# A linear-attention block with a gated FFN on one core: another search for the order of the instructions, and the last sum in two halves of columns

## The chip, the cores and the metric

The kernel runs on one core of a Trainium2 chip. The time is the device time of one execution in microseconds (us); the median of three runs before the change is 631.77 us (631.66 to 632.82). The core has a matrix engine (TensorE, in rows PE, its weight loads PEld), VectorE (DVE), ScalarE (ACT), GpSimd (POOL), and SyncE (SP), whose queue issues all DMA transfers. Every engine works off its own instructions in a fixed order, and waits at the first one whose inputs aren't ready.

## The reference

With x of 2048 tokens by 512, xn = layernorm(x), 32 heads of 16, F = 1792, all float32:

```
q, k, v = split(xn @ wqkv);  phi(t) = where(t > 0, t + 1, exp(t)) + 1e-6
kv = phi(k)^T v per head;  z = sum of phi(k) over the tokens
s = (phi(q) kv / (phi(q) z + 1e-6)) @ wo
g = silu((gelu(xn @ w_gate) * (xn @ w_up)) @ w_down)
out = x + s * g
```

## The kernel before, in words

**Products.** Each float32 product is computed as three matmuls on operands split into a rounded high part and a low part (hi·hi, hi·lo, lo·hi: `mm3`, L362 to L366). The high part is a cast on ScalarE (L350), the low part a subtraction, mostly on VectorE (L356). Block products are done in a seven-product form with fewer products and more sums; the sums of x blocks (`forms`, tiles T0 to T7) and of weight blocks (`prep_w`, tiles tmp) are GpSimd additions of 128x256, those of outputs (c, u, e) VectorE additions.

**Stages.** Tokens come in 16 tiles of 128 rows, taken in pairs (0 with 4, 1 with 5, and so on). From 0 to about 100 us: load x and wqkv, layernorm (`ln`, L496: statistics st, mv and ve on VectorE, rstd on GpSimd, xn on VectorE), transposition on TensorE (pt, L522), high and low parts of x (Xh, Xl) and of weights (kq, a21, b12), then k and q. phi of k (kp) and of q (qp) is made from two ScalarE steps and a VectorE step (L591); q goes to DRAM (q_d), and xn^T phi(k) is summed up in four PSUM banks (gps). The first raw FFN weights (raw0, raw1) and the spills of Xh and Xl to DRAM (xh_d, xl_d) go over the same SP queue from about 40 us on. Then the FFN runs for the second half of the tokens (FX, FY, FZ; fu, h, hh, hl; the down sums d into acc), the attention of all tiles follows at 356 to 410 us (u = phi(q)·z on GpSimd, den and its reciprocal rr and pn on VectorE, ptq by transposition, pqTh on ScalarE, pqTl on VectorE, sps = 12 products a tile), then the FFN of the first half. Its last down sums (`down`, L868) end the kernel: per j of 8, 12 products into one PSUM bank of 128x512, an addition to acc (L885), silu (L895), a multiplication with s (L1069), an addition of x, and a transfer out (`finish0`, L1060). Already before, j=7 did the steps behind the products in two halves of 256 columns; the sums of x for j < 6 were GpSimd's.

**What sets the order.** The program states the operations once. Its class `Plan` gives each a cost, finds what it depends on (tiles, PSUM banks, buffer places), and lists them: `forward` (L205) walks in time and takes on each engine the ready operation with the smallest due time `late`; TensorE's operations are bound to a stated order within 6 us. Due times come from eight passes back from the end (`latest`, L178). After that 400 rounds (`ROUNDS`, L19 and L134) each draw a wait of TensorE, shift the due times of operations around it at random, list again, and keep what ends sooner by the planner's own account. That account holds one port that GpSimd operations and VectorE operations without PSUM operands take in turns, and one DMA line at 260 KB/us with 1.5 us on top. The order so found is what each engine gets.

Of the kernel before, what the change touches and what calls it, by code (L numbers as in the profile page):

```python
# [18 lines left out]
ROUNDS = 400  # L19
# [50 lines left out]
class Op:  # L70
    __slots__ = ("eng", "cost", "lat", "fn", "pre", "suc", "key", "late", "end", "left", "ready", "name", "turn", "port", "kb", "lat0")


class Plan:

    AHEAD = 6.0
    RATE = 260.0
# [5 lines left out]
    def do(self, eng, cost, fn, out, *ins, more=(), lat=0.0, key=None, name="", kb=0):  # L83

        op = Op()
        op.eng, op.cost, op.lat, op.key, op.name = eng, cost, lat + self.HOP[eng], key, name
# [24 lines left out]
        for p in op.pre:  # L111
            p.suc.append(op)
        self.ops.append(op)
        return op

    def order(self, pe_keys):
        rank = {k: i for i, k in enumerate(pe_keys)}
        pe = sorted((o for o in self.ops if o.eng == "PE"), key=lambda o: rank[o.key])
        now = 0.0
        for o in pe:  # L120
            o.turn = now
            now += o.cost
# [10 lines left out]
        draw = random.Random(1)  # L133
        for n in range(ROUNDS):  # L134
            end, done, late = best
            for o in self.ops:
                o.late = late[o]
            waits = self.waits(done)
            at = draw.choices([w[0] for w in waits], [w[1] for w in waits])[0]
            back, share, far = draw.uniform(1.0, 12.0), draw.choice((0.05, 0.2, 0.5)), draw.uniform(0.2, 4.0)  # L140
# [3 lines left out]
            done = self.forward(pe)  # L144
            end = max(t for t, _ in done)
            if end <= best[0]:
                best = end, done, {o: o.late for o in self.ops}
        return [o for _, o in best[1]]

    @staticmethod  # L150
    def waits(done):

        out, last = [], 0.0
        for t, o in done:
            if o.eng == "PE":
                if t - o.cost - last > 0.02:
                    out.append((o.late, t - o.cost - last))
                last = t
        out.append((last, max(t for t, _ in done) - last - 4.0))
        return out  # L160
# [44 lines left out]
    def forward(self, pe):  # L205
# [8 lines left out]
        done, first = [], 0  # L214
        while any(cands.values()):
# [3 lines left out]
            for e, c in cands.items():  # L219
# [46 lines left out]
def kernel(  # L266
# [52 lines left out]
    def U(tag, places, name, dtype=F32, shape=(P, D)):  # L319
        return tile_in("up", ring(tag, places), list(shape), dtype, name)  # L320
# [137 lines left out]

    load_next()
# [33 lines left out]

    xns = {}

    def ln(*ts):  # L496
        n = len(ts)
        mv = little("mv", f"mv{ts[0]}", [P, n, 2])
        for i, t in enumerate(ts):
            st = little("st", f"st{t}", [P, 6])  # L500
            do("DVE", 0.6, lambda o, i: nc.vector.bn_stats(o, i), st, xs[t]).port = False
            do("DVE", 0.1, lambda o, i: nc.vector.bn_aggr(o, i), mv[:, i], st)
        ve = little("ve", f"ve{ts[0]}", [P, n])
        do("DVE", 0.1, lambda o, i: nc.vector.tensor_scalar_add(o, i, EPS_LN), ve, mv[:, :, 1])
        rstd = little("rs", f"rstd{ts[0]}", [P, n])
        do("POOL", 0.6, lambda o, i, j: nc.gpsimd.tensor_tensor(o, i, j.to_broadcast([P, n]), op=ALU.pow),
           rstd, ve, neg_half)
        for i, t in enumerate(ts):
            xns[t] = U("xn", range(4, 9), f"xn{t}")
            do("DVE", 0.46, lambda o, i, m, r: nc.vector.tensor_scalar(o, i, m, r, op0=ALU.subtract, op1=ALU.mult),  # L510
               xns[t], xs.pop(t), mv[:, i, 0:1], rstd[:, i:i + 1], name=f"xn{t}")
# [163 lines left out]
    for n in range(NP):  # L675
        if n == 0:
            for t in tokens[n]:
                ln(t)
# [188 lines left out]

    def down(p, units_, is_first, is_last, finish):  # L868
        for j in range(8):
            key = (11, 21) if j < 4 else (12, 22)  # L870
            sl = slice((j % 4) * P, (j % 4 + 1) * P)
            ps = bank(ring("down", [5, 6, 7]), f"d{p}_{units_[0]}_{j}")
            for n, u in enumerate(units_):
                for i in range(2):
                    def run(o, hh, hl, dh, dl, sl=sl, i=i, st=(n == 0 and i == 0), sp=(n == len(units_) - 1 and i == 1)):
                        mm3(o, hh[:, sl], hl[:, sl], dh[:, i], dl[:, i], st, sp)
                    do("PE", 0.68, run, ps, *hs[p, u, key[i]], *dws[p, u], key=("D", p, u, j, i), name="down")
            if is_first:
                acc[p, j] = tile_in("up", FACC[j], [P, D], F32, f"acc{p}_{j}")
                copy("ACT", acc[p, j], ps, D, "acc")  # L880
            else:
                n = 2 if p == 0 and is_last and j == 7 else 1
                for i in range(n):
                    cl = (slice(None), slice(i * D // n, (i + 1) * D // n))
                    do("DVE", dve(D // n), lambda o, i: nc.vector.tensor_add(o, o, i), acc[p, j][cl], ps[cl], name="acc")  # L885
# [5 lines left out]
    def silu(p, j, n=1):  # L891
        w = D // n
        for i in range(n):
            cl = (slice(None), slice(i * w, (i + 1) * w))
            do("ACT", act(w), lambda o: nc.scalar.activation(o, o, AF.Silu), acc[p, j][cl], name="silu")  # L895

    def ffn(p, finish):
# [15 lines left out]
        def down_keys(g):  # L913
            for j in range(8):
                keys.extend(("D", p, u, j, i) for u in g for i in range(2))
# [13 lines left out]
        return keys, lambda j: [("D", p, u, j, i) for u in todo[0] for i in range(2)]  # L929
# [42 lines left out]
    do("DVE", 0.59, lambda o, i: nc.vector.tensor_reduce(o, i, axis=AX.X, op=ALU.add), den_eps, zb3)  # L972
# [27 lines left out]
    def attn(i):  # L1000
# [6 lines left out]
        do("DVE", 0.59, lambda o, i: nc.vector.tensor_reduce(o, i, axis=AX.X, op=ALU.add), den, heads(u), name="den")  # L1007
        do("DVE", 0.2, lambda o, i: nc.vector.tensor_add(o, o, i), den, den_eps)
        r = little("rr", f"rr{t}", [P, H])
        do("DVE", 0.28, lambda o, i: nc.vector.reciprocal(o, i), r, den)  # L1010
# [49 lines left out]
    def finish0(p, j):  # L1060
        n = 2 if j == 7 else 1
        sr, xr = U("fs", [*FG, *FX], f"fs{j}"), U("fxr", [*FE, *FC], f"fx{j}")
# [4 lines left out]
        for i in range(n):  # L1067
            cl = (slice(None), slice(i * w, (i + 1) * w))
            do("DVE", dve(w), lambda o, a: nc.vector.tensor_mul(o, o, a), sr[cl], acc[p, j][cl])  # L1069
            tt("POOL" if j < 6 else "DVE", "add", sr[cl], sr[cl], xr[cl], w)  # L1070
            dma(ext(out[j * P:(j + 1) * P, i * w:(i + 1) * w]), sr[cl], 256 // n)
# [34 lines left out]
```

## Time and profile before

| | us |
|---|---|
| median of 3 runs | 631.77 |
| profiled execution | 629.64 |
| span of its trace | 627.6 |
| TensorE busy | 616.1 (98%) |
| VectorE busy | 422.2 (67%) |
| ScalarE busy | 321.2 (51%) |
| GpSimd busy | 247.9 (40%) |
| last product of TensorE starts | 620.68 |

Busy shares are averages over stages with different limits, so the stretches count. TensorE's granted clock is shown at full speed all through, but for the last stretch, in which it has no products. A matmul's shown end is modelled, so the shown products overlap; from start to start they are nearer to the engine's real pace.

### The profile page before, as it was taken

The numbers are of one execution on the slowest core, as the hardware profiler recorded it, in microseconds if no ns is written. First come the engines' busy times: TensorE is split into PE (matmuls) and PEld (weight loads), VectorE is DVE, ScalarE is ACT, GpSimd is POOL, SyncE is SP. The second block draws the span as 40 slices with busy tenths as digits, with TensorE's granted clock in tenths as the row PEclk, the third lists the DMA queues.
The fourth block names the chain that finished last, engine by engine and source line by source line (L and its number), as shares of the span: only waits on it lengthen the run. The fifth ranks groups of instructions, "written<-read, shape, count | busy, mean of one in ns | idle before, by whom it ended". The sixth has DMA issues, their size and how long they took to land.

```text
span 627.6 us, 7822 instructions
## 1 busy us (share of the span) xinstructions
PE 616.1 (98%) x2780; PEld 506.0 (81%) x2780; DVE 422.2 (67%) x644; ACT 321.2 (51%) x571; POOL 247.9 (40%) x243
## 2 busy tenths in 40 slices
PE   7999999999999999999999999999999999999995
PEld 6878788888888888888888787888888888888884
DVE  6999998688746743762459689967566527723554
ACT  6677777797565622650345322266656316612431
POOL 2465554456644530360035433135534404300142
PEclk9999999999999999999999999999999999999999
DMA  6239921136121210220069544872221202000173
GB/s 239 80 124 299 298 68 38 65 102 201 44 72 54 56 46 34 67 68 0 34 201 359 199 131 148 289 251 67 68 65 36 68 34 68 0 1 34 34 206 130
DMA packets 52439, 68.67 MB, mean 109 GB/s; under 512 B 2864, under 2 KB 31792, under 8 KB 52400
## 3 DMA queue, kind: packets, MB, share of 16 engines
q1 hardware_dynamic: 52400, 68.17, 33.9%
q8 instruction: 22, 0.36, 0.2%
q14 instruction: 17, 0.14, 0.1%
HBM read 49.28 MB, written 18.87 MB: 109 GB/s over the span
## 4 chain that ended last, share of the span: by engine, by line
PE 94%; DVE 3%; ACT 1%; issue 0%; POOL 0%; DVEq 0%; ACTq 0%; POOLq 0%
PE FX L364 8%; PE FX L365 8%; PE FX L366 8%; PE d L365 8%; PE d L366 8%; PE d L364 8%; PE FZ L365 4%; PE FZ L366 4%; PE FZ L364 4%; PE sps L366 2%; PE sps L364 2%; PE sps L365 2%; PE gps L366 2%; PE gps L364 2%; PE gps L365 2%; PE FY L365 2%
## 5 line engine op out<-in xcount | busy, mean ns | idle before, releaser
L847 POOL TENSOR_TENSOR h<-h,g 128x512 f32<-128x512 f32 x42 | 62.1, 1477 | 173.3 <-DVE h L356 173.3
L364 PE MATMUL d<-dwh,hh 128*128 128x512 f32 x224 | 87.8, 392 | 0.0
L364 PE MATMUL FX<-Xh,w 128*128 128x512 f32 x224 | 87.5, 391 | 0.1
L366 PE MATMUL FX<-Xh,w 128*128 128x512 f32 x224 | 87.2, 389 | 0.0
L366 PE MATMUL d<-dwh,hl 128*128 128x512 f32 x224 | 87.2, 389 | 0.0
L365 PE MATMUL d<-dwl,hh 128*128 128x512 f32 x224 | 87.2, 389 | 0.0
L365 PE MATMUL FX<-Xl,w 128*128 128x512 f32 x224 | 87.2, 389 | 0.0
L356 POOL TENSOR_TENSOR tmp<-raw 128x256 f32<-128x256 f32 x56 | 49.1, 890 | 85.1 <-DVE w L356 70.3
L885 DVE TENSOR_TENSOR acc<-acc,d 128x512 f32<-128x512 f32 (+1 forms) x49 | 32.8, 674 | 52.5 <-PE d L366 52.1
L350 ACT COPY fu<-FX 128x512 f32<-128x512 f32 x56 | 32.9, 587 | 54.3 <-PE FX L366 53.7
L350 ACT CAST hh<-h 128x512 fp32r<-128x512 f32 x56 | 34.5, 620 | 46.4 <-PE d L365 27.0
L364 PEld LDWEIGHTS FX<-Xh,w 128*128 128x128 f32 x224 | 42.0, 188 | 10.0 <-ACT fu L350 1.4
L364 PEld LDWEIGHTS d<-dwh,hh 128*128 128x128 f32 x224 | 42.1, 188 | 8.9 <-issue 0.2
L365 PEld LDWEIGHTS d<-dwl,hh 128*128 128x128 f32 x224 | 42.1, 188 | 8.8 <-issue 0.2
L366 PEld LDWEIGHTS d<-dwh,hl 128*128 128x128 f32 x224 | 42.0, 188 | 8.7
L366 PEld LDWEIGHTS FX<-Xh,w 128*128 128x128 f32 x224 | 42.0, 188 | 8.7
L365 PEld LDWEIGHTS FX<-Xl,w 128*128 128x128 f32 x224 | 42.0, 188 | 8.7
L356 DVE TENSOR_TENSOR w<-tmp,w 128x512 fp32r<-128x512 f32 x56 | 42.0, 772 | 9.8 <-ACT w L350 9.8
L356 DVE TENSOR_TENSOR w<-raw,w 128x512 fp32r<-128x512 f32 (+1 forms) x56 | 45.7, 825 | 3.2 <-ACT w L350 3.2
L356 DVE TENSOR_TENSOR hl<-h,hh 128x512 fp32r<-128x512 f32 x56 | 41.2, 735 | 5.6 <-ACT hh L350 5.6
L364 PE MATMUL FZ<-Xh,w 128*128 128x512 f32 x112 | 43.6, 389 | 0.0
L365 PE MATMUL FZ<-Xl,w 128*128 128x512 f32 x112 | 43.6, 389 | 0.0
(186 smaller groups left out, 1396.8 us busy)
## 6 DMA issues: line engine op xcount, KB each, us to landing
raw<-in_B_w_gate SPq DMA_DIRECT2D x14, 512.0 KB, 3.8
raw<-in_B_w_up SPq DMA_DIRECT2D x14, 512.0 KB, 3.8
draw<-in_B_w_down SPq DMA_DIRECT2D x14, 512.0 KB, 3.3
x<-in_A_x SPq DMA_DIRECT2D x16, 256.0 KB, 3.3
q_d<-qp SPq DMA_DIRECT2D x16, 256.0 KB, 2.2
q<-q_d SPq DMA_DIRECT2D x16, 256.0 KB, 3.0
xh_d<-Xh SPq DMA_DIRECT2D x4, 896.0 KB, 5.9
xl_d<-Xl SPq DMA_DIRECT2D x4, 896.0 KB, 6.4
```

The costliest lines, as they stand in the source:

```text
L350: do("ACT", act(n), lambda o, i: nc.scalar.copy(o, i), dst, src, name=name)
L356: do(eng, c, lambda o, p, q: getattr(e, f"tensor_{op}")(o, p, q), dst, a, b, name=name)
L364: nc.tensor.matmul(ps, wh, mh, start=start, stop=False, skip_group_check=on)
L365: nc.tensor.matmul(ps, wh, ml, start=False, stop=False, skip_group_check=on)
L366: nc.tensor.matmul(ps, wl, mh, start=False, stop=stop, skip_group_check=on)
L847: do("POOL", pool(NC), lambda o, i: nc.gpsimd.tensor_mul(o, o, i), h, g, name="h")
L885: do("DVE", dve(D // n), lambda o, i: nc.vector.tensor_add(o, o, i), acc[p, j][cl], ps[cl], name="acc")
```

## The change

The table `KEPT` replaces the 400 rounds: each line names a stretch of TensorE's turn and the seeds whose alterations are applied in it, one after the other, with no comparison at run time (`altered`). Half of the alterations now bring forward the chain of operations that held up a wait (`chain`). The planner's account counts ScalarE's table loads (`LOAD`), gives the port to whoever asked first and takes a little off an operation that had to wait for it (`CUT`), frees some VectorE operations of the port (`port=False`), and has other rates for DMA (`RATES`, `RATE`, 0.9 us on top). The program states the first tile's layernorm ahead of the weight splits. For j = 7 of the last sum, `halves` is 2: its 24 products are stated as two runs of 12, each of 256 columns, into two PSUM banks. The additions of x at the end for j < 6 go from GpSimd to VectorE. ScalarE's activation table loads are five in both kernels.

```diff
-ROUNDS = 400
+KEPT = [
+    (-1, 12, [10, 19, 22, 51, 67, 152]),
...
+    (605, 9999, [30]),
+]
+TABLES = {"exp": "exp", "gelu": "gelu", "silu": "silu"}
+LOAD = 1.28
+RATES = 215.0, 380.0
...
-    RATE = 260.0
+    RATE = 220.0
+    CUT = {"DVE": 0.13, "POOL": 0.04}
...
-        op.port = eng == "POOL" or eng == "DVE" and cost > 0.25 and not any(
+        op.port = eng == "POOL" or eng == "DVE" and port and not any(
...
+        for lo, hi, draws in KEPT:
+            for n in draws:
+                best = self.altered(n, lo, hi, pe, *best)
+        return [o for _, o in best[1]]
+
+    def altered(self, n, lo, hi, pe, _, done, late):
+        draw = random.Random(n)
+        for o in self.ops:
+            o.late = late[o]
+        waits = [w for w in self.waits(done) if lo <= w[0] < hi]
...
+        w = draw.choices(waits, [w[1] for w in waits])[0]
+        if draw.random() < 0.5:
+            for o in self.chain(done, w[2]):
+                if draw.random() < 0.7:
+                    o.late -= draw.uniform(0.0, 4.0)
+        else:
...
-                if best is None or t < best[0]:
-                    best = t, o
-            t, o = best
+                asked = max(free[e], o.ready)
+                if best is None or (t, asked) < best[:2]:
+                    best = t, asked, o
+            t, asked, o = best
             cands[o.eng].remove(o)
-            free[o.eng] = t + o.cost
-            o.end = t + o.cost
+            if o.table and o.table != table:
+                t, table = t + LOAD, o.table
+
+            took = o.cost - (min(self.CUT[o.eng], t - asked) if o.port else 0.0)
+            free[o.eng] = o.end = t + took
...
-                dma = max(dma, o.end) + o.kb / self.RATE
-                o.lat = dma - o.end + 1.5
+                dma = max(dma, o.end) + o.kb / (RATES[0] if o.end < 3.0 else RATES[1])
+                o.lat = max(dma - o.end, o.kb / self.RATE) + 0.9
...
+    ln(tokens[0][0])
     for k in range(2):
         kq_split(0, wk1, k)
...
         if n == 0:
-            for t in tokens[n]:
-                ln(t)
+            ln(tokens[n][1])
...
+    def halves(p, units_, j):
+        return 2 if p == 0 and units_ == groups[-1] and j == 7 else 1
...
+            for c in range(m):
+                ps = bank(ring("down", [5, 6, 7]), f"d{p}_{units_[0]}_{j}{c}", (P, D // m))
+                cs = slice(c * D // m, (c + 1) * D // m)
...
+                            mm3(o, hh[:, sl], hl[:, sl], dh[:, i, cs], dl[:, i, cs], st, sp)
...
-            tt("POOL" if j < 6 else "DVE", "add", sr[cl], sr[cl], xr[cl], w)
+            tt("DVE", "add", so, so, xr[:, i * w:(i + 1) * w], w)
```

What the new order looks like is seen at three places. In the names, the number before the underline belongs to the token tile or the weight unit.

**The start, VectorE.** x4 is the second x tile; Xl0 takes the low part of the transposed first tile, kq0 the low part of the first key weights. Before:

```order
L510 TENSOR_SCALAR xn0_149<-x0_95,mv0_140,rstd0_145 128x512
L501 BN_STATS st4_152<-x4_110 128x6
L502 BN_AGGR mv4_163<-st4_152 128x2
L504 TENSOR_SCALAR ve4_167<-mv4_163 128x1
L356 TENSOR_TENSOR Xl0_170<-pt0_154,Xh0_165 128x2x128 x2
L510 TENSOR_SCALAR xn4_177<-x4_110,mv4_163,rstd4_172 128x512
L356 TENSOR_TENSOR kq0_175<-wk1_106,kq0_175 128x512 x2
```

After:

```order
L523 BN_STATS st4_141<-x4_113 128x6
L532 TENSOR_SCALAR xn0_149<-x0_95,mv0_133,rstd0_139 128x512
L524 BN_AGGR mv4_153<-st4_141 128x2
L526 TENSOR_SCALAR ve4_158<-mv4_153 128x1
L532 TENSOR_SCALAR xn4_171<-x4_113,mv4_153,rstd4_165 128x512
L413 TENSOR_TENSOR kq0_173<-wk1_117,kq0_173 128x512 x2
L413 TENSOR_TENSOR Xl0_190<-pt0_160,Xh0_169 128x2x128 x2
```

st4 goes ahead of xn0, and xn4 directly behind ve4; the Xl subtractions go behind the first two of kq. On SP's queue the transfer of x4 goes from third place (behind the first wk) to second.

**About 55 to 65 us, VectorE and GpSimd.** T3 holds the sums of x blocks of the fourth pair, Xl0<-T3 their low parts, tmp0 the sums of the first gate weights raw0. VectorE before:

```order
L356 TENSOR_TENSOR Xl0_170<-T3_701,Xh0_165 128x4x128
L591 SCALAR_TENSOR_TENSOR qp6_729<-c22_2_656,qr6_676 128x512
L510 TENSOR_SCALAR xn8_736<-x8_408,mv8_487,rstd8_507 128x512
L510 TENSOR_SCALAR xn12_741<-x12_422,mv8_487,rstd8_507 128x512
L356 TENSOR_TENSOR xnl6_751<-xn6_415,xnh6_568 128x512
L356 TENSOR_TENSOR c11_3_757<-e1_3_734,Y3_704 128x512
L591 SCALAR_TENSOR_TENSOR kp6_762<-c12_2_715,kr6_739 128x512
L501 BN_STATS st13_773<-x13_627 128x6
L356 TENSOR_TENSOR Xl0_170<-T3_701,Xh0_165 128x4x128
```

After:

```order
L413 TENSOR_TENSOR c11_3_737<-e1_3_728,Y3_694 128x512
L413 TENSOR_TENSOR Xl0_190<-T3_711,Xh0_169 128x4x128
L524 BN_AGGR mv9_748<-st9_679 128x2
L524 BN_AGGR mv9_748<-st13_723 128x2
L649 SCALAR_TENSOR_TENSOR kp6_757<-c12_2_691,kr6_740 128x512
L413 TENSOR_TENSOR Xl0_190<-T3_711,Xh0_169 128x4x128
L413 TENSOR_TENSOR xnl6_778<-xn6_463,xnh6_566 128x512
L532 TENSOR_SCALAR xn8_797<-x8_425,mv8_524,rstd8_787 128x512
```

Between the two Xl0<-T3 seven instructions stood, now three; the xnl and one of the xn stand behind. GpSimd in the same stretch, before:

```order
L356 TENSOR_TENSOR T2_559<-xt2_457 128x256
L356 TENSOR_TENSOR T2_559<-xt2_457,T2_559 128x256
L602 TENSOR_TENSOR zacc_108<-zacc_108,kp2_637 128x512
L356 TENSOR_TENSOR T1_672<-xt1_308 128x256 x2
L356 TENSOR_TENSOR T3_701<-xt3_661 128x256
L356 TENSOR_TENSOR T3_701<-xt3_661,T3_701 128x256
```

After:

```order
L528 TENSOR_TENSOR rstd3_589<-ve3_586,neg_half_97 128x2
L660 TENSOR_TENSOR zacc_115<-zacc_115,kp2_623 128x512
L413 TENSOR_TENSOR tmp0_677<-raw0_626 128x256 x2
L413 TENSOR_TENSOR tmp0_677<-tmp0_677,raw0_626 128x256
L413 TENSOR_TENSOR T3_711<-xt3_640 128x256
L413 TENSOR_TENSOR T3_711<-xt3_640,T3_711 128x256
```

The T1 sums ahead of T3 are replaced by three sums tmp0, which read raw0; rstd3 stands right ahead of zacc. On SP's queue two of the spills of Xh and Xl stand further ahead of raw0. At about 43 us, VectorE's qp5 stood behind kq subtractions of 1024 and 512 columns and an xnl; in the new order these stand behind qp5.

**Attention at about 387 us, TensorE.** ptq4 and ptq13 are the transpositions of pn of tiles 4 and 13, sps12 and sps4 the products behind them. Before:

```order
L366 MATMUL sps12_3645<-M_hi_3298,pqTl12_3634 128x512
L1019 MATMUL ptq4_3671<-ident_90,pn4_3643 128x128 x4
L1019 MATMUL ptq13_3676<-ident_90,pn13_3665 128x128 x4
L364 MATMUL sps4_3694<-M_hi_3298,pqTh4_3682 128x512
L365 MATMUL sps4_3694<-M_lo_3301,pqTh4_3682 128x512
```

After:

```order
L422 MATMUL sps3_3655<-M_lo_3325,pqTh3_3632 128x512
L423 MATMUL sps3_3655<-M_hi_3319,pqTl3_3641 128x512
L1080 MATMUL ptq4_3681<-ident_90,pn4_3635 128x128 x4
L421 MATMUL sps12_3688<-M_hi_3319,pqTh12_3669 128x512
L422 MATMUL sps12_3688<-M_lo_3325,pqTh12_3669 128x512
```

ptq4 goes from a place beside ptq13, behind the twelve sps12, to one ahead of them. On VectorE, in this stretch, den and pn stand 5 to 14 rows further ahead, pqTl 8 to 14 rows further back, and two subtractions of 1024 columns (the low parts of the first down weights, dwl0) are taken in.

Of the rest of TensorE's order: six products d of a down sum, not three, stand ahead of the last FX block; and the last twelve products are now 24 of half the width.

## Rows read from the trace of the kernel before

**Rows 1.** The page's chain of waits: share of the span by engine.
```profile
PE 94%; DVE 3%; ACT 1%; issue 0%; POOL 0%; DVEq 0%; ACTq 0%; POOLq 0%
```

**Rows 2.** Waits of TensorE by releaser: us in total, times, longest.
```profile
PE pt L522 <- DVE xn L510: 2.0, 1, 2.0
...
PE X L366 <- DVE Xl L356: 0.4, 1, 0.4
```

**Rows 3.** Table of stretches: busy us of each engine, clock, DMA share, GB/s.
```profile
45.00:66.00 21.00, 20.57 (x95) 16.28 (x94) 19.43 (x32) 13.89 (x25) 9.06 (x11) 1.00 0.97 295
66.00:100.00 34.00, 34.00 (x158) 27.89 (x158) 33.13 (x52) 25.67 (x48) 21.22 (x20) 1.00 0.46 139
356.00:410.00 54.00, 53.71 (x267) 43.89 (x265) 48.51 (x86) 15.41 (x26) 14.48 (x11) 1.00 0.58 193
```

**Rows 4.** Timeline of the end: start, us, engine, line, operation, tiles, [idle before].
```profile
618.18 0.39 PE L364 MATMUL d<-dwh,hh 128*128 128x512 f32 x1
618.87 0.19 PEld L365 LDWEIGHTS d<-dwl,hh 128*128 128x128 f32 x1
...
620.68 0.39 PE L366 MATMUL d<-dwh,hl 128*128 128x512 f32 x1
621.17 0.74 DVE L885 TENSOR_TENSOR acc<-acc,d 128x256 f32<-128x256 f32 x2
622.58 0.42 DVE L356 TENSOR_TENSOR fs<-fs,fx 128x256 f32<-128x256 f32 x1
623.37 0.42 DVE L356 TENSOR_TENSOR fs<-fs,fx 128x256 f32<-128x256 f32 x1
```

**Rows 5.** Timeline around 44, VectorE and TensorE.
```profile
41.73 1.75 DVE L356 TENSOR_TENSOR kq<-wq,kq 128x1024 fp32r<-128x1024 f32 x1
43.41 0.68 DVE L591 SCALAR_TENSOR_TENSOR qp<-q,qr 128x512 f32<-128x512 f32 x1
44.14 0.50 PE L364 MATMUL Y<-kq,Xh 128*128 128x512 f32 x1 [0.53 <-DVE qp L591]
```

**Rows 6.** Timeline of the start: SP's queue, VectorE, TensorE.
```profile
1.24 0.42 SPq L346 DMA_DIRECT2D wk<-in_A_wqkv  x1
...
6.23 0.69 DVE L501 BATCH_NORM_STATS2 st<-x 128x6 f32<-128x512 f32 x1 [0.49 <-DMA x<-in_A_x]
8.64 0.66 PE L522 MATMUL pt<-ident,xn 128*128 128x128 f32 x4 [1.98 <-DVE xn L510]
```

**Rows 7.** Transfers by issue: KB each, median us from issue to landing.
```profile
wk<-in_A_wqkv SPq DMA_DIRECT2D x1, 256.0 KB, 3.1
...
raw<-in_B_w_gate SPq DMA_DIRECT2D x1, 512.0 KB, 8.4
```

**Rows 8.** Timeline from 48 to 61: SP's queue and GpSimd.
```profile
48.42 3.52 SPq L346 DMA_DIRECT2D raw<-in_B_w_gate  x1
...
55.74 0.74 POOL L356 TENSOR_TENSOR T<-xt 128x256 f32<-128x256 f32 x1 [1.24 <-ACT xt L350]
57.94 3.04 POOL L356 TENSOR_TENSOR T<-xt,T 128x256 f32<-128x256 f32 x3
```

**Rows 9.** Timeline in attention, TensorE.
```profile
387.64 1.03 PE L1019 MATMUL ptq<-ident,pn 128*128 128x128 f32 x8
388.97 0.50 PE L364 MATMUL sps<-M_hi,pqTh 128*128 128x512 f32 x1 [0.29 <-ACT pqTh L350]
```

**Rows 10.** Timeline at 597: weight load of FX.
```profile
596.97 0.19 PEld L364 LDWEIGHTS FX<-Xh,w 128*128 128x128 f32 x1 [0.47 <-ACT fu L350]
```

**Rows 11.** Timeline at 346: 24 fp32 products of 128 columns.
```profile
345.86 2.84 PE L979 MATMUL pkv<-mstuff 128*128 128x128 f32 x24
```

**Rows 12.** Timeline in attention: VectorE beside GpSimd, and alone.
```profile
368.27 1.32 POOL L356 TENSOR_TENSOR u<-q,mstuff 128x512 f32<-128x512 f32 x1 [3.22 <-DMA q<-q_d]
368.37 1.77 DVE L1012 SCALAR_TENSOR_TENSOR pn<-q,rr 128x512 f32<-128x512 f32 x1
...
371.86 0.69 DVE L1012 SCALAR_TENSOR_TENSOR pn<-q,rr 128x512 f32<-128x512 f32 x1
```

More of the change, by code (lines that the diff above doesn't have):

```diff
@@ L70 @@
 class Op:
-    __slots__ = ("eng", "cost", "lat", "fn", "pre", "suc", "key", "late", "end", "left", "ready", "name", "turn", "port", "kb", "lat0")
+    __slots__ = ("eng", "cost", "lat", "fn", "pre", "suc", "key", "late", "end", "left", "ready", "name", "turn", "port", "kb", "lat0", "no", "table")
 class Plan:
     AHEAD = 6.0
-    RATE = 260.0
+    RATE = 220.0
+    CUT = {"DVE": 0.13, "POOL": 0.04}
     HOP = {"PE": 0.21, "ACT": 0.15, "DVE": 0.13, "POOL": 0.09, "SP": 0.0}
@@ L81, in __init__, with do @@
         self.ops = []
-    def do(self, eng, cost, fn, out, *ins, more=(), lat=0.0, key=None, name="", kb=0):
+    def do(self, eng, cost, fn, out, *ins, more=(), lat=0.0, key=None, name="", kb=0, port=True):
         op = Op()
+        op.no, op.table = len(self.ops), TABLES.get(name)
         op.eng, op.cost, op.lat, op.key, op.name = eng, cost, lat + self.HOP[eng], key, name
@@ L131, in order @@
                 best = end, done, {o: o.late for o in self.ops}
[L133 to L140, printed above, removed]
+        for lo, hi, draws in KEPT:
[7 more added lines that the diff above has]
+        waits = [w for w in self.waits(done) if lo <= w[0] < hi]
+        if not waits:
+            return _, done, late
+        w = draw.choices(waits, [w[1] for w in waits])[0]
[4 more added lines that the diff above has]
+        else:
+            at, back = w[2].late, draw.uniform(1.0, 12.0)
+            share, far = draw.choice((0.05, 0.2, 0.5)), draw.uniform(0.2, 4.0)
             for o in self.ops:
@@ L143, in order @@
                     o.late += draw.uniform(-far, far)
[L144 to L148, printed above, removed]
+        new = self.forward(pe)
+        return max(t for t, _ in new), new, {o: o.late for o in self.ops}
     @staticmethod
@@ L156, in waits, with chain @@
                 if t - o.cost - last > 0.02:
-                    out.append((o.late, t - o.cost - last))
+                    out.append((o.turn, t - o.cost - last, o))
                 last = t
-        out.append((last, max(t for t, _ in done) - last - 4.0))
+        t, o = max(done, key=lambda d: d[0])
+        out.append((o.turn, t - last, o)) if o.eng == "PE" else out.append((1000.0, t - last, o))
+        return out
+    def chain(self, done, o):
+        end = {q: t for t, q in done}
+        for q in self.ops:
+            q.lat = q.lat0 + q.kb / self.RATE
+        before, last = {}, {}
+        for t, q in done:
+            before[q] = last.get(q.eng)
+            last[q.eng] = q
+        out = []
+        for _ in range(14):
+            out.append(o)
+            held = [(end[q] + self.gap(q, o), q) for q in o.pre]
+            if before[o]:
+                held.append((end[before[o]], before[o]))
+            if not held:
+                break
+            o = max(held, key=lambda h: (h[0], h[1].no))[1]
         return out
@@ L213, in forward @@
                 cands[o.eng].append(o)
-        done, first = [], 0
+        done, first, table = [], 0, "exp"
         while any(cands.values()):
@@ L317, in ring, with U, columns @@
         return places[n % len(places)]
-    def U(tag, places, name, dtype=F32, shape=(P, D)):
-        return tile_in("up", ring(tag, places), list(shape), dtype, name)
+    def U(tag, places, name, dtype=F32, shape=(P, D), parts=1):
+        return tile_in("up", ring(tag, places), list(shape), dtype, name, parts)
+    def columns(v, i, n):
+        w = D // n
+        return v.part(v.res if n == 1 else v.res[i:i + 1], (slice(None), slice(i * w, (i + 1) * w)))
     def little(tag, name, shape):
@@ L914, in down_keys @@
             for j in range(8):
-                keys.extend(("D", p, u, j, i) for u in g for i in range(2))
+                keys.extend(("D", p, u, j, i, 0) for u in g for i in range(2))
         todo = [list(g) for g in groups]
@@ L928, in ffn @@
         assert len(todo) == 1
-        return keys, lambda j: [("D", p, u, j, i) for u in todo[0] for i in range(2)]
+        return keys, lambda j: [("D", p, u, j, i, c) for c in range(halves(p, todo[0], j)) for u in todo[0] for i in range(2)]
     keys1, last1 = ffn(1, lambda p, j: silu(p, j))
@@ L1060, in finish0 @@
     def finish0(p, j):
[L1061 to L1062 removed]
+        n = halves(p, groups[-1], j)
+        sr = U("fs", [*FG, *FX], f"fs{j}", parts=n)
+        xr = U("fxr", [*FE, *FC], f"fx{j}")
         dma(sr, s_d(j, slice(j * P, (j + 1) * P)), 256)
```

87 lines of the change are left out of this document (45 added, 42 removed).

## The prediction

> **What bounds the kernel now.** I read the chain of waits first: TensorE has 94% of the chain that ended last, VectorE 3% [rows 1]. A change that leaves every product in place can only win where TensorE stands still, or behind its last product. The waits of TensorE by releaser say where: one transposition stood 2.0 us behind a normalised x tile, X 0.4 us behind Xl [rows 2], and below come Y, sps and FX. The stretches then say who is short of time: VectorE works 19.43 of 21.0 us from 45 to 66 while the DMA engines are busy to 0.97, 33.13 of 34.0 from 66 to 100, and 48.51 of 54.0 in attention, 356 to 410 [rows 3]. There, a VectorE instruction that is displaced comes back as a wait; in the long FFN stretches it does not.
>
> A wait costs more than the idle time shown. The last sum's twelve products start 0.227 us apart (618.18 to 620.68, 11 steps) and each is shown as 0.39 us [rows 4], so 0.16 us of a gap hides under the shown end of the product before; and the product behind a wait is shown as 0.50 us [rows 5], 0.11 longer. Price of a wait: idle + 0.27 us.
>
> **Start.** The order takes x4 from the third place on SP's queue to the second. The piece of wk in second place was issued at 1.24 [rows 6] and landed 3.1 us later [rows 7], at 4.34; VectorE, idle for x4, could begin its statistics only at 6.23 [rows 6]. x4 lands 1.9 us earlier. From statistics to transposition (8.64) went 2.41 us [rows 6]; from about 4.55 that is 6.96. The first tile's normalisation comes in between and two Xl pieces go out, so I put it at 7.3, 1.3 us earlier. Against that, the wk piece that gave way lands as late as x4 did, 1.9 us later, and k needs its high and low parts. Of the 1.3 I take +0.5, nearer to zero since VectorE's queue behind it is full; ends −0.6 (a third of wk's delay comes through to k) and +1.3.
>
> **Y at 44.** qp is issued at 43.41, right behind a kq subtraction of 1.75 us begun at 41.73, and Y starts at 44.14 after 0.53 us of idle [rows 5]. In the new order that subtraction, one of 512 columns and an xnl stand behind qp. Worth 0.53+0.27 = 0.80 us; they must still be done somewhere, so I take +0.6; ends 0 and 0.8.
>
> **X at 64.8.** Idle 0.4, so about 0.7. X waits for the second Xl of T3. GpSimd had begun T3 at 55.74, after 1.24 us without work, and 57.94+3.04 ends its last form and two T1 forms [rows 8]; so the late one is VectorE's queue, where two xn, an xnl and a statistics stand ahead of that Xl. The new order moves these behind it or to long before: good for the 0.7. But on GpSimd it puts three tmp0 additions ahead of T3, and they need raw0, the first gate weights. raw0 was issued at 48.42 [rows 8] and took 8.4 us [rows 7], to 56.8, while the DMA engines had no room. At 0.74 us each, as T's of the same size [rows 8], raw0 must land by 55.74−2.2 = 53.5 for T3 to begin when it did. Two of the spills go earlier in the new order, and I expect raw0 at about that moment. I take +0.4; upper end 0.7, lower −3.3 (landing as before: T3 at 59.0).
>
> **Attention.** At 387.64 the transpositions of two tiles run in a row, and sps then waits 0.29 us for the first one's cast [rows 9]. The new order sets ptq4 twelve products ahead. That takes away 0.29+0.27 = 0.56 if pn4 is done by then, and pn too stands further ahead on VectorE. I take +0.5; ends 0 and 0.56.
>
> **FFN.** One wait that the list by releaser doesn't show: FX's weight load at 596.97 stood 0.47 us behind the copy fu [rows 10], 0.24 more than a product's 0.227; with the 0.11 of the restart 0.35. In the new order six products of a down sum, not three, come in between. I take +0.3 and no more, since VectorE's and ScalarE's queues here are the same; ends 0 and 0.35.
>
> **End.** The last sum becomes two runs of 12 products with 256 columns. Before, the first half's addition at 621.17 waited for the last product (620.68), though it reads only its own columns, and the last addition ended at 623.37+0.42 = 623.79 [rows 4]. No row shows a product of 256 columns. Half of 0.227 is 0.114; 24 fp32 products of 128 columns, each with its weight load, took 2.84 us, 0.118 each [rows 11]; the weight load is shown as 0.19 [rows 4], and 24 of these are 4.6 us. I take 0.12, the pkv row's, since there too every product has its own weights: 2.88 us against 12 x 0.227 = 2.72, so TensorE ends 0.16 later. What is left behind it is the second half alone: from addition to sum a half needs 622.58+0.42−621.17 = 1.83 us [rows 4]; from 621.33, with 0.2 us for what VectorE still has of the first half and of j=6, 623.36. Gain 0.43; I take +0.35; ends −1.5 (at 0.19 each) and 0.45. Six fs additions that GpSimd did go to VectorE: 0.69 us each (pn's, of the same 128x512 [rows 12]), one to each 2.72 us of products, beside an addition and a multiplication of the same length: 2.07 of 2.72, so hidden. If the cover were gone, only j=6's would count, and its 0.69 stands ahead of the second half's multiplication already.
>
> The Trainium skill, "TensorE: Matmul & The Clock Gate", section "LDWEIGHTS (loading the stationary operand)", gives a weight load as its columns divided by 1.2 in ns: 107 ns for 128, not the 0.19 us shown. By it the halves cost what I took; by the row taken as a pace they would cost 1.8 us of TensorE. pkv's 0.118 agrees with the page.
>
> **New waits.** In attention VectorE gets two low-part subtractions of 1024 columns from the FFN (at most 1.4 us each, twice pn's 0.69), and pqTl stands 8 to 14 rows nearer to its use. A VectorE instruction that meets a GpSimd one is drawn out: pn took 1.77 us beside u's 1.32, and 0.69 alone [rows 12]. A meeting costs 1.1 us. Some will be new, and some of today's will go; I allow −1.0 for one that reaches TensorE, in attention or between 66 and 100; ends 0 and −2.2 (two).
>
> The Trainium skill, "SBUF — State Buffer", section "SBUF: two separate sides", speaks of a port pair of VectorE and GpSimd that one of them locks for a whole instruction while the other is blocked. pn's 1.08 us on top fits inside u's 1.32. By that rule a meeting could cost up to 1.3 and two of them 2.6, 0.4 beyond my end.
>
> **Sum.** 0.5+0.6+0.4+0.5+0.3+0.35−1.0 = 1.65 us. The profiled execution took 629.64 us (span 627.6 and 2.04 around it), so 628.0 after. The median of the runs shown is 631.77, 2.13 above it; with the same distance, 630.1. This case's own range is 628.5 to 631.5, from a meeting more or less and half of each gain. A measurement here can't tell under 0.2%, 1.26 us, from no change.
>
> **Rivals.**
> *No change that can be measured* (0.22): the same waits go, but VectorE, busy to 97% from 66 to 100, gives the start and Y back and two meetings cost 2.2: 0+0+0.4+0.5+0.3+0.35−2.2 = −0.65, 632.4. For it: the full stretches [rows 3]. Against: each removed wait stands behind VectorE work that has a later use.
> *GpSimd stuck on raw0* (0.14, slower): if raw0 lands at 56.8 as before, T3 begins 3.3 us late, Xl stands at the head of VectorE's queue for as long, and the full stretch behind can't catch up: −3.3 in place of +0.4, sum −2.05, 633.8. It decides from a landing at about 55.5, where the loss of 2.0 eats the rest of the gain. For it: DMA at 0.97. Against: the earlier spills.
> *Weight loads pace the halves* (0.06): −1.5 in place of +0.35, sum −0.2, 632.0.
> *No new wait* (0.18): 2.65 to 4.2 (all upper ends), 629.1 to 627.6, say 628.5. For it: nothing in the FFN stretches, where TensorE never stood, is made tighter.
> The forecast has 0.40.
>
> **How the numbers follow.** Faster by over 0.2% (under 630.5): two thirds of the forecast's 0.40, 0.18 of the lucky case, and 0.12 of the others where one of their terms doesn't come: 0.57. Slower (over 633.0): 0.11 of the raw0 case and 0.04 of the no-change case: 0.15. Same: 0.28. The range, 627.4 to 633.2, holds all but most of the raw0 case and the far end of the lucky one.
>
> **What would show it.** In the new profile: the second transposition starts by 7.4 and not after 2 us of idle; Y no longer waits for qp near 44; tmp0 begins before 54 and T3 by 56.5; sps does not wait near 387; at the end 24 products 0.12 apart, and 2.1 to 2.3 us rather than 2.7 from the last product's end to the last addition's. The forecast is wrong if tmp0 begins after 56, if TensorE's new waits add up to over 1.5 us, or if the halves' products stand 0.15 us or more apart.

## The result, and the profile after

The changed kernel takes 633.72 us (median of 15 runs), the kernel before 631.65 us in as many runs beside it: ratio 1.0041, interval 1.0026 to 1.0056. It is 0.4% slower; 630.1 with 627.4 to 633.2 was forecast. The profiled execution took 632.71 us with a span of 630.8, so 3.1 us more than before, against the medians' 2.1. Both kernels have runs with a lower granted clock that take some 2 us more (last section); with the higher clock alone the medians are 633.2 for the changed kernel and 630.4 to 630.6 for the kernel before in the rounds below, 2.6 to 2.8 us apart, and both profiles are of such runs.

The waits of TensorE by releaser in the profile after (us in total, times, longest), to be laid beside [rows 2]:

```profile
PE sps L423 <- DVE pqTl L413: 1.2, 2, 0.7
PE warm L444 <- DVE neg_half L435: 1.1, 1, 1.1
PE k L423 <- DVE Xl L413: 0.8, 1, 0.8
PE X L421 <- ACT Xh L407: 0.7, 1, 0.7
PE X L423 <- DVE Xl L413: 0.5, 1, 0.5
PE k L422 <- DVE kq L413: 0.5, 2, 0.3
PE pt L580 <- DVE xn L532: 0.3, 1, 0.3
```

The transposition's 2.0 us and Y's wait are gone, as forecast. In their place stand waits that the kernel before did not have: sps for pqTl twice, X for Xh, and at the start k for Xl and for kq, 1.3 in sum (before, k waited 0.5 for b). X waits for Xl as before. The stretches of [rows 3] after the change (busy us of TensorE, its weight loads, VectorE, ScalarE and GpSimd, then clock, DMA share, GB/s):

```profile
45.00:66.00 21.00, 19.60 (x87) 15.09 (x87) 18.56 (x31) 13.99 (x25) 11.78 (x12) 1.00 0.87 260
66.00:100.00 34.00, 34.00 (x158) 27.11 (x157) 30.64 (x53) 24.94 (x47) 21.39 (x20) 1.00 0.54 160
356.00:410.00 54.00, 52.63 (x258) 42.07 (x258) 45.95 (x83) 16.75 (x29) 13.53 (x10) 1.00 0.60 208
```

VectorE is less busy than before in all three (18.56 for 19.43, 30.64 for 33.13, 45.95 for 48.51), and yet TensorE stands still for 1.4 us in the first and 1.4 in the third, where before it was 0.4 and 0.3. So the rows do not speak for too much work on VectorE; who stood still at which moment, a busy share can't show.

Where the time went is seen when the starts of TensorE's products are laid side by side: at the same amount of work done (each product at its start-to-start length), how much later is the kernel after (its lag)?

| place in the kernel before, us | lag of the kernel after, us |
|---|---|
| 19.7 | +0.3 |
| 40.0 | +0.5 |
| 50.8 (behind Y) | −0.1 |
| 61.4 | +0.8 |
| 92.7 | +1.7 |
| 333.7 | +1.9 |
| 386.5 (in attention) | +4.3 |
| 397.8 | +3.8 |
| 558.4 | +4.0 |
| 618.8 (last products) | +3.6 |
| end of the last addition | +3.1 |

Two steps make the loss: 1.8 us between 51 and 93, 2.4 us in attention. All else is a gain of 1.1 in sum.

**First step: GpSimd and raw0.** SP's queue, GpSimd and TensorE from 48 to 65:

```profile
48.60 0.53 SPq L403 DMA_DIRECT2D xl_d<-Xl  x1
49.22 1.76 SPq L403 DMA_DIRECT2D raw<-in_B_w_gate  x1
...
56.65 1.44 POOL L413 TENSOR_TENSOR tmp<-raw 128x256 f32<-128x256 f32 x2 [5.27 <-DMA raw<-in_B_w_gate]
59.20 1.24 POOL L413 TENSOR_TENSOR T<-xt 128x256 f32<-128x256 f32 x1
64.89 1.16 POOL L528 TENSOR_TENSOR rstd<-ve,neg_half 128x2 f32<-128x2 f32 x1
...
61.96 0.50 PE L421 MATMUL X<-kq,Xh 128*128 128x512 f32 x1 [0.74 <-ACT Xh L407]
```

raw0 is issued 0.8 us later than before [rows 8], behind a spill of 896 KB, and GpSimd stands 5.27 us at the head of its queue until it has landed. This spill, xl_d, stands directly ahead of raw0 in the kernel before too:

```profile
47.82 0.51 SPq L346 DMA_DIRECT2D xl_d<-Xl  x1
```

It goes out as soon as VectorE has written Xl, and that was 0.8 us later in the new order (48.57 for 47.79). Only then come three tmp0 sums, then T3 (59.20, before 55.74), two of T1, and rstd at 64.89, and X waits for the cast of T3's first forms.

**Second step: VectorE and q.** GpSimd, VectorE and TensorE at 365 to 387:

```profile
365.51 1.29 POOL L413 TENSOR_TENSOR u<-q,mstuff 128x512 f32<-128x512 f32 x1 [8.24 <-DMA q<-q_d]
366.84 0.69 DVE L1068 TENSOR_REDUCE den<-u 128x32 f32<-128x512 f32 x1 [2.97 <-POOL u L413]
368.76 0.68 DVE L413 TENSOR_TENSOR pqTl<-ptq,pqTh 128x512 fp32r<-128x512 f32 x1
369.50 0.50 PE L423 MATMUL sps<-M_hi,pqTl 128*128 128x512 f32 x1 [0.70 <-DVE pqTl L413]
...
383.71 2.32 DVE L1073 SCALAR_TENSOR_TENSOR pn<-q,rr 128x512 f32<-128x512 f32 x2
385.95 0.68 DVE L413 TENSOR_TENSOR pqTl<-ptq,pqTh 128x512 fp32r<-128x512 f32 x1
386.68 0.50 PE L423 MATMUL sps<-M_hi,pqTl 128*128 128x512 f32 x1 [0.55 <-DVE pqTl L413]
```

u waits 8.24 us for the transfer of q. den, which reads u, stands at the head of VectorE's queue and waits 2.97 us with it; behind it stand two additions and then pqTl, whose inputs were long there, and sps waits 0.70. At 383.71 two pn, one of them beside a GpSimd u, take 2.32 us ahead of another pqTl: 0.55.

**The end.** The rows that answer to [rows 4]:

```profile
621.83 0.28 PE L421 MATMUL d<-dwh,hh 128*128 128x256 f32 x1
...
624.58 0.28 PE L423 MATMUL d<-dwh,hl 128*128 128x256 f32 x1
623.46 0.42 DVE L948 TENSOR_TENSOR acc<-acc,d 128x256 f32<-128x256 f32 x1 [0.75 <-PE d L423]
624.90 0.42 DVE L948 TENSOR_TENSOR acc<-acc,d 128x256 f32<-128x256 f32 x1
626.18 0.75 DVE L413 TENSOR_TENSOR fs<-fs,fx 128x256 f32<-128x256 f32 x2
```

24 products start within 2.75 us (23 steps of 0.1196). From the start of the last one to the end of the last addition 624.58 to 626.93 are 2.35 us, where before it were 3.11.

### The profile page after: what moved, and what is told of

It is laid out like the page before. It is cut to its first block, busy times and chain, and to the rows that moved or that the text cites. A ratio compares the mean times of both kernels' runs of the same rounds, so it can differ in the third digit from the quotient of the medians.

```text
span 630.8 us, 7851 instructions
## 1 busy us (share of the span) xinstructions
PE 619.3 (98%) x2792; PEld 506.5 (80%) x2792; DVE 420.4 (67%) x650; ACT 321.0 (51%) x571; POOL 235.4 (37%) x237
## 5 line engine op out<-in xcount | busy, mean ns | idle before, releaser
L904 POOL TENSOR_TENSOR h<-h,g 128x512 f32<-128x512 f32 x42 | 60.4, 1439 | 176.9 <-DVE h L413 176.7
L421 PE MATMUL d<-dwh,hh 128*128 128x512 f32 (+1 forms) x228 | 88.4, 388 | 0.0
L422 PE MATMUL d<-dwl,hh 128*128 128x512 f32 (+1 forms) x228 | 87.9, 385 | 0.0
L423 PE MATMUL d<-dwh,hl 128*128 128x512 f32 (+1 forms) x228 | 87.9, 385 | 0.0
L413 POOL TENSOR_TENSOR tmp<-raw 128x256 f32<-128x256 f32 x56 | 44.3, 805 | 95.6 <-DVE w L413 70.1
L413 DVE TENSOR_TENSOR w<-raw,w 128x512 fp32r<-128x512 f32 (+1 forms) x56 | 47.1, 847 | 3.4 <-ACT w L407 3.3
L423 PE MATMUL FZ<-Xh,w 128*128 128x512 f32 x112 | 43.6, 389 | 0.0
L421 PE MATMUL FZ<-Xh,w 128*128 128x512 f32 x112 | 43.6, 389 | 0.0
```

The lines of the kernel that those rows point to most:

```text
L413: do(eng, c, lambda o, p, q: getattr(e, f"tensor_{op}")(o, p, q), dst, a, b, name=name)
L421: nc.tensor.matmul(ps, wh, mh, start=start, stop=False, skip_group_check=on)
L422: nc.tensor.matmul(ps, wh, ml, start=False, stop=False, skip_group_check=on)
L423: nc.tensor.matmul(ps, wl, mh, start=False, stop=stop, skip_group_check=on)
L904: do("POOL", pool(NC), lambda o, i: nc.gpsimd.tensor_mul(o, o, i), h, g, name="h")
```

## The experiments

All kernels below but three are the changed kernel with some instructions moved within the queues of one or more engines, after the planner has given its list; the products, the tiles and SP's queue stay as they are. Fences that begin with an engine's name list its order and are no code. Each was run beside the kernel before, and ratios are to it.

**T3 ahead of tmp0.**

```diff
 GpSimd:  zacc
-         tmp0, tmp0, tmp0
          T3, T3, T3, T3
+         tmp0, tmp0, tmp0
          T1, T1, rstd8, T1, T1
```

> The changed kernel with three GpSimd instructions moved: the tmp0 sums, which read the first gate weights raw0, stand behind the four T3 sums instead of ahead of them. Nothing else differs. Theory (the head of GpSimd's queue waited 5.27 us for raw0's transfer, and T3, Xh and Xl stood behind it): T3 begins at about 57.2, when xt is copied, instead of 59.20; the waits of X for Xh (0.7) and Xl (0.5) near 61 and 62 go; TensorE comes out of the first 100 us about 1.5 us earlier, and the time falls by 1.5, to about 1.1 us (0.17%) above the kernel before. Rival (VectorE is full from 66 to 100 and decides there whatever T3 does): the two waits go, but others of the same sum come up before 100, and the time falls by less than 0.4 us.

Measured 1.0045 (1.0031 to 1.0060): no gain. X's waits are gone, and T3 begins at 57.24, but a transposition now waits. GpSimd, VectorE and TensorE of this run:

```profile
57.24 0.74 POOL L432 TENSOR_TENSOR T<-xt 128x256 f32<-128x256 f32 x1 [5.81 <-ACT xt L426]
61.11 2.38 POOL L432 TENSOR_TENSOR tmp<-raw 128x256 f32<-128x256 f32 x2
66.56 0.70 POOL L547 TENSOR_TENSOR rstd<-ve,neg_half 128x2 f32<-128x2 f32 x1
67.31 0.94 DVE L551 TENSOR_SCALAR xn<-x,mv,rstd 128x512 f32<-128x512 f32 x1 [2.11 <-POOL rstd L547]
68.39 0.30 PE L599 MATMUL pt<-ident,xn 128*128 128x128 f32 x1 [1.93 <-DVE xn L551]
```

rstd stands behind tmp0 and T1, xn behind rstd, pt behind xn. The loss had moved from T3 to the next thing in GpSimd's queue; in this profile the stretch from 51 to 93 costs 3.0 us. The rival's outcome came, other waits and no gain, but for another reason: it named the wrong engine, since VectorE stood idle for 2.11 us here. The theory was too narrow (T3).

**Attention: three moves on VectorE.**

```diff
 VectorE: pqTl, pn
-         den (its u waits for q)
          acc, acc, pqTl
+         den
 ...
+         pqTl
          pn
-         pqTl
```

(the second place twice, for the tiles at 386 and 399)

> The changed kernel with three VectorE moves in attention: the sum den of the tile whose q came in late stands behind the next pqTl instead of at the head of the queue; one pqTl goes ahead of the second of two pn; one pqTl goes ahead of a pn. Theory (pqTl stood behind VectorE instructions that waited for a transfer or were drawn out by GpSimd, and sps behind it): the pqTl waits near 369 and 386 (0.7 and 0.55) go with their restarts, and the small one at 399; the stretch from 356 to 410 is passed some 1.8 us sooner, the time falls by 1.8. Rival (VectorE has simply more to do there, the two dwl among it): the waits move to the next sps, and the time falls by less than 0.5 us.

Measured 1.0020 (1.0004 to 1.0036): 1.3 us less than the changed kernel, but the two intervals overlap, so the time alone does not show a gain. No wait of sps is left in the list of this run; but pm waited 1.1 us for mstuff at 353, by the same pattern one stage ahead. VectorE and TensorE of this run:

```profile
349.48 0.69 DVE L1087 TENSOR_REDUCE den<-u 128x32 f32<-128x512 f32 x1 [2.32 <-POOL u L432]
...
353.11 0.68 DVE L1062 TENSOR_TENSOR mstuff<-pkv,mask 128x512 f32<-128x512 f32 x1
353.85 0.70 PE L1071 MATMUL pm<-mstuff 128*128 128x512 f32 x1 [1.11 <-DVE mstuff L1062]
```

den waits for u (and u for q), and mstuff, the masked copy of pkv that pm needs, stands five instructions behind.

**Both.** 

> Both sets of moves on the changed kernel. Theory: the two gains are in different stretches and add up, 3.3 us, so 0.5 to 1 us below the kernel before. Rival: less than 1 us in sum, so still over 1.5 us above the kernel before.

Measured 1.0022 (1.0009 to 1.0036), as the attention moves alone; the T3 half brought nothing here either.

**The two halves in turns.**

```diff
 TensorE: d of j=7
-         first half x12, second half x12
+         first x3, second x3, first x3, second x3, ...
```

> The changed kernel with the products of the two halves of the last sum in turns (three of the one, three of the other), so that both halves end together, as in the kernel before, while each product stays 256 columns wide. It takes away only the early end of the first half. Theory (the early half is what shortens the end): from the start of the last product to the end of the last addition 2.9 to 3.1 us, as before, instead of 2.35, the time 0.5 us longer than the changed kernel's. Rival (VectorE's own queue of ten instructions sets the end): the same 2.35 to 2.5 us and no difference.

Measured 1.0038 (1.0017 to 1.0058): by the time alone it can't be told from the changed kernel. The trace tells it: the last product starts at 627.89, and the rows of the last addition are

```profile
627.89 0.28 PE L442 MATMUL d<-dwh,hl 128*128 128x256 f32 x1
630.40 0.75 DVE L432 TENSOR_TENSOR fs<-fs,fx 128x256 f32<-128x256 f32 x2
```

so 3.26 us behind the last product for 2.35. In the eight profiles with the changed kernel's order at the end it is 2.34 or 2.35 us. The early first half does give back 0.9 us behind the last product.

**All of GpSimd's queue ahead of tmp0.**

```diff
 GpSimd:  zacc
-         tmp0, tmp0, tmp0
          T3, T3, T3, T3
-         T1, T1, rstd8, T1, T1
+         rstd8, T1, T1, T1, T1
+         tmp0, tmp0, tmp0
```

> The changed kernel with four GpSimd instructions moved: behind the zacc sum come the four T3 sums, then rstd8, then the four T1 sums, and only then the tmp0 sums that read raw0. In the run before this one only T3 was put ahead of tmp0; X's waits went, but rstd8 still stood behind tmp0, xn behind rstd8, and a transposition waited 1.9 us for xn at 66. Theory (everything that stands behind the wait for raw0 in GpSimd's queue pays, whichever it is): with all of it ahead, X's waits and the transposition's are both gone, TensorE is 1.5 to 1.8 us ahead of the changed kernel at 100 us, and the time is 0.1 to 0.2% above the kernel before instead of 0.4. Rival (VectorE is too full in this stretch, whatever GpSimd does): another wait of 1 to 2 us before 100, ratio to the kernel before 1.004 again.

Measured 1.0014 (0.9999 to 1.0028): 1.7 us less than the changed kernel, with intervals that just touch, and no wait of X or pt between 45 and 70. GpSimd of this run:

```profile
57.96 0.74 POOL L438 TENSOR_TENSOR T<-xt 128x256 f32<-128x256 f32 x1 [5.82 <-ACT xt L432]
67.06 1.18 POOL L438 TENSOR_TENSOR tmp<-raw 128x256 f32<-128x256 f32 x1
```

In its profile the stretch from 51 to 93 costs 0.8 us instead of 1.8. The theory in its wider form holds: the wait for raw0 at the head of the queue cost 1.0 us by the profiles and 1.7 by the medians, whoever stood behind it. The other 0.8 of this stretch is left in every profile of this order; its cause was not tried.

**The same with four moves on VectorE:** the three in attention, and mstuff.

```diff
 VectorE: den, rr, den
+         mstuff
          pn, rr, den
-         mstuff
```

> The same with the three VectorE moves in attention, and a fourth: the copy mstuff of pkv, ahead of pn and den at 349, since it stood behind a den that waited for q's transfer (pm then waited 0.1 to 1.1 us in the runs so far). Theory: gains add, 1.6 + 1.3 + 0.5 us, so 0.8 us or 0.1% below the kernel before, ratio 0.998 to 1.000. Rival: 1.002 or more, as with the attention moves alone.

Measured 0.9979 (0.9966 to 0.9992): the gains add, 3.9 us below the changed kernel and below the kernel before. Against the run above, the attention part is 2.2 us, and here the intervals lie apart.

**The start alone.**

```diff
 ScalarE:
-         xnh, Xh, kq0, kq0, b, Xh
+         kq0, xnh, kq0, Xh, Xh, b
 VectorE:
-         xn4, kq0 lo, kq0 lo, Xl, Xl
+         kq0 lo, xn4, Xl, kq0 lo, Xl
```

> The changed kernel with the start alone put in another order: ScalarE casts the first two kq before xnh and Xh, VectorE does the first low part before xn4 and the first Xl between two low parts. Theory (k waits for Xl, 0.8, and twice for kq, 0.3, because the casts stand behind steps of x though their weights have landed): these three waits shrink by 1 us or more in sum, TensorE reaches 12 us about 1 us ahead; VectorE, nearly full behind, gives back half, so the time falls by 0.5 us. Rival (VectorE's work to 45 us is the bound): the waits move to 12 to 30 us, no difference.

Measured 1.0034 (1.0019 to 1.0049): no difference that can be told. In its profile k's wait for Xl is 0.9 instead of 0.8, and the two for kq are 0.5 in sum as before; the waits did not shrink, and the theory falls; nor did they move to 12 to 30 us, as the rival said. This run also shows that the loss in attention varies: its order there is the changed kernel's, and yet no sps waits in its list, but pm 1.0 us for mstuff.

**All the moves.** 

> All the moves on the changed kernel: GpSimd's, VectorE's in attention, and the start. Theory: the sum of the three, 3.5 to 4 us below the changed kernel, so 1 us (0.2%) below the kernel before, ratio 0.997 to 0.999. Rival: at or above the kernel before.

Measured 0.9973 (0.9961 to 0.9985), 629.61 us median: 1.7 us below the kernel before, the lowest median here, though its interval overlaps that of the run with eight moves (0.9979). Its waits of TensorE:

```profile
PE pt L615 <- DVE xn L567: 1.2, 1, 1.2
PE warm L479 <- DVE neg_half L470: 1.1, 1, 1.1
PE k L458 <- DVE Xl L448: 0.9, 1, 0.9
PE k L457 <- DVE kq L448: 0.5, 2, 0.3
PE X L456 <- DVE qp L684: 0.4, 1, 0.4
```

Behind 14 us there is nothing but one of 0.4.

**The planner's old account of transfers.**

```diff
-                dma = max(dma, o.end) + o.kb / (RATES[0] if o.end < 3.0 else RATES[1])
-                o.lat = max(dma - o.end, o.kb / self.RATE) + 0.9
+                dma = max(dma, o.end) + o.kb / 260.0
+                o.lat = dma - o.end + 1.5
```

> The changed kernel with one part undone: the planner's account of transfers is the old one (260 KB/us in line and 1.5 us on top; not 215 and 380 KB/us and 0.9). All else stays, the 24 kept alterations too, though they now work on another list. In the order it gives, GpSimd has tmp0 behind T3, rstd8 and T1. Theory (the account lets transfers land too early, so instructions that read them were put at the head of queues): no wait of 1 us for raw0's consumers between 55 and 70, less waiting in attention, and the time falls by 1 to 3 us against the changed kernel, ratio 0.999 to 1.002. Rival (the seeds were kept for the new account, and with another one they spoil as much as they mend): 1.003 or more.

Measured 1.0037 (1.0024 to 1.0050), so the rival's time. Both have a part of it. GpSimd's order is the good one: T3 at 57.47, rstd at 62.75, tmp0 only at 65.64:

```profile
57.47 1.12 POOL L413 TENSOR_TENSOR T<-xt 128x256 f32<-128x256 f32 x1 [3.56 <-ACT xt L407]
...
62.75 1.08 POOL L528 TENSOR_TENSOR rstd<-ve,neg_half 128x2 f32<-128x2 f32 x1
...
65.64 0.92 POOL L413 TENSOR_TENSOR tmp<-raw 128x256 f32<-128x256 f32 x1
```

and in attention no sps waits for pqTl and no den for u. In the next run, with the new account and without the alterations, tmp0 stands ahead of T3 and den waits for u twice (3.1 and 2.9 us near 360 and 365). So the account of transfers is what put the tmp0 sums and den at the heads of the queues. But Y waits for qp again (0.6 at 47), X for a copy u (1.0 at 69), and the start is slower by over 1 us. That the kept seeds were drawn for another list would explain it, but is not shown.

**Without the kept alterations.**

```diff
-KEPT = [
-    (-1, 12, [10, 19, 22, 51, 67, 152]),
...
+KEPT = []
```

> The changed kernel without the kept alterations: the list of the eight passes stands as it is, with the new account of transfers. GpSimd has tmp0 ahead of T3 here too. Theory (the account, not the alterations, brings the loss): the wait for raw0 near 52 to 57 on GpSimd and those of X or a transposition behind it are there, and the time is that of the changed kernel or up to 3 us longer, ratio 1.004 to 1.009. Rival (the alterations made the loss): faster than the changed kernel, ratio under 1.003.

Measured 1.0156 (1.0139 to 1.0172), more than the theory's 1.009. GpSimd waits for raw0 here too:

```profile
58.72 1.83 POOL L403 TENSOR_TENSOR tmp<-raw 128x256 f32<-128x256 f32 x2 [3.98 <-DMA raw<-in_B_w_gate]
```

so the alterations didn't bring that wait in. They are worth 7 us on the chip, of which some 5 are a lower clock (last section). The rival falls.

**The six additions back on GpSimd,** on the kernel with all moves.

```diff
-            tt("DVE", "add", so, so, xr[:, i * w:(i + 1) * w], w)
+            e = nc.vector if j > 5 else nc.gpsimd
+            do("DVE", dve(w), lambda o, a, b, e=e: e.tensor_add(o, a, b), so, so, xr[:, i * w:(i + 1) * w])
```

> The kernel with all the moves, and the six additions fs of the end (j from 0 to 5) given back to GpSimd. Prediction's step (those six are hidden on either engine): no difference from the kernel with all the moves, ratio 0.996 to 0.999, the last product to the end of the last addition 2.35 us as there. Rival (GpSimd's slower addition holds the port against VectorE's, or its transfers go out late): 0.5 us or more longer behind the last product.

Measured 0.9982 (0.9972 to 0.9993), which overlaps the 0.9973; from the last product to the last addition's end 2.35 us again. So the six are hidden on either engine. The profiled run has a wait of sps for pqTl in attention, 1.2 us, where the order is that of the run above, which had none: from one execution to the next that place still varies; what made the difference was not looked into.

## Why the prediction was wrong

- **X at 64.8 is the step that failed first.** It put raw0's landing "at about that moment", 53.5, and took +0.4. raw0 was issued later, not earlier, and landed at 56.6, as in the kernel before (56.8): two of the spills did go out earlier, but the one directly ahead of raw0 did not. The stretch from 51 to 93 cost 1.8 us, of which 1.0 to 1.7 go with tmp0 behind. The prediction had this as its slower rival, with 0.14, at 633.8; T3 began at 59.20 where the rival said 59.0. But the rival's price of 3.3 was about twice too high: without tmp0 ahead T3 began only at 57.24, when xt was cast, so raw0 delayed it by 2.0 us, and TensorE had other products until 61. It hit the time, 633.7, by luck, because attention lost as much again. The lower end of the step was in the range; its chance was the mistake. With the DMA engines 0.97 busy [rows 3] and a spill just ahead in SP's queue, nothing in the trace spoke for a landing 3 us earlier. Two of the prediction's own signs of being wrong came: tmp0 began after 56, at 56.65, and the new waits of TensorE add up to over 1.5 us (1.2 of sps and 0.7 of X alone).
- **New waits and Attention.** The ptq4 step was right: the lag falls from 4.3 to 3.8 there, 0.5 as forecast. The new waits were mis-sized and had the wrong cause. They were priced as meetings of VectorE and GpSimd, at 1.0; one of that kind came (two pn in 2.32 us, 0.55 of idle). The larger, in this profile, was a den that waits for u, and u for the transfer of q, ahead of a pqTl that was ready. In sum attention lost 2.4 before ptq4 gave 0.5 back; the moves give back 2.2. The size varies: over the five profiles with the changed order there, the lag grows from 345 to 398 by 0.7 to 2.7 us, ptq4's gain taken off. The order had shown den 5 to 14 rows further ahead; the prediction read that as slack for pn, and did not ask what den itself waits for.
- **Start.** +0.5 was forecast, −0.3 to −0.5 came. The second transposition did start earlier (7.46 against 8.64), but k waited 0.78 for Xl and twice for kq. The lower end, −0.6, named that. Part of it is chance: the warm-up's products, which run ahead of the first transposition, start 0.21 us apart at first and 0.11 later, and that change came at 4.3 us in the kernel before and at 5.3 after. In the seven profiles with the new start it came between 4.25 and 6.8, and the lag at 19.7 follows it without exception, from −0.0 (at 4.25) to +1.1 (at 6.8). With the change as early as in the kernel before, the new start thus gains and loses nothing.
- **Y.** +0.6 forecast; the lag goes from +0.5 to −0.1, so the step was right.
- **FFN.** +0.3 forecast; the lag falls by 0.35 at 597, and by 0.2 at 425, but new waits of FX for fu give it back (the lag rises by 0.3 at 165 and by 0.25 around 540). Net nothing.
- **End.** +0.35 forecast; from the first product of the last sum to the end of the last addition 5.61 us became 5.10, so 0.5. The products' 0.12 was right (0.1196). The Trainium skill gives 107 ns for a weight load of 128 columns ("TensorE: Matmul & The Clock Gate", section "LDWEIGHTS (loading the stationary operand)"), by which loads don't pace the halves; the trace agrees, with 0.1196 us a product where the shown loads of 0.19 would have made it more.
- Taken together: with the two queues put right, the kernel is 1.3 us below the kernel before by the medians (0.9979); the terms without new waits were 2.65 (0.5+0.6+0.4+0.5+0.3+0.35). At the higher clock alone it is 0.2 us (630.2 to 630.4), and its profile is 0.3 us shorter: all its 12 runs have that clock, and 14 of the 35 of the kernel before beside them have not. So Y, ptq4 and the end came, but the start and the FFN gave nothing, and by this comparison most of the 1.3 us is the lower clock of those 14 runs.

## What to carry to other kernels

On an engine that works in order, an instruction that waits for a transfer is charged to everything behind it. So when a new order moves such an instruction ahead, look first at what it reads and at when the last such transfer landed in the trace; if the DMA engines are busy there, take the old landing time as the likely one. And when a repair only moves the wait to the next in the queue, the head of the queue is the cause, not the one that was seen waiting.

## What the runs showed of the hardware

A wait can cost more than its length. In the profile of the kernel with the halves in turns, whose order at 60 us is that of the changed kernel, X waited 1.0 and 0.55 us near 61 and 63, and then the granted clock fell to about half; TensorE's products then started 0.43 us apart instead of 0.227 (columns as in the stretches above):

```profile
60.00:62.00 2.00, 1.61 (x8) 0.99 (x6) 1.09 (x2) 0.26 (x2) 1.92 (x3) 1.00 1.05 347
62.00:64.00 2.00, 0.84 (x3) 0.41 (x4) 1.41 (x4) 1.97 (x4) 2.00 (x3) 1.00 0.20 74
64.00:66.00 2.00, 2.00 (x5) 1.55 (x6) 2.00 (x2) 1.58 (x4) 1.92 (x3) 0.53 0.25 73
66.00:68.00 2.00, 2.00 (x7) 1.62 (x6) 2.00 (x4) 1.48 (x3) 2.00 (x3) 0.62 0.97 278
68.00:70.00 2.00, 2.00 (x11) 1.57 (x10) 0.82 (x1) 0.54 (x2) 2.00 (x3) 1.00 1.00 288
```

That is the lower of the engine's two levels, 1.2 for 2.4 GHz; it had been busy for 0.84 of the 2 us before. From the two shares the fall cost some 1.7 us ((1−0.53)·2 + (1−0.62)·2, an estimate). In the changed kernel's own profile the same two waits, of 0.74 and 0.54 us, were followed by no such fall. Nor was the single wait of 2.0 us at the start of the kernel before, in its profile, nor that of 1.93 us in the run with T3 ahead. The kernel without the kept alterations showed the fall twice, at 12 to 15 us (share 0.53, behind waits of 0.9 and 0.3) and at 66 to 72 us (0.50, behind waits of 1.1 and 1.9); with the edges, 0.90 from 9 to 12 and 0.79 from 72 to 74, that is 5.1 us by the same estimate.

The runs show it as well. Of the 87 of the kernel before in the three rounds of experiments, 36 have a granted clock of 0.995 or 0.996 over the whole run and took 631.9 to 633.2 us; the others, at 0.997 to 0.999, took 629.7 to 631.4. Of the changed kernel's 15, 4 are at 0.995 or 0.996, with 635.0 to 637.4; the others took 632.2 to 634.3. The kernel with all the moves has none of 12 below 0.997, and against the higher group of the kernel before its gain is 0.8 us, not 1.7. Where the clock falls in those runs no profile shows, and why the fall comes in one run and not in another was not tried.
